# Three chained stages on one Trainium2 core: operands of the last stage at equal addresses mod 512, and its first tiles split inside the middle stage

## The chip, the cores and the metric

The kernel runs on one core of one Trainium2 chip. The metric is device time in microseconds (us) of one execution; the times of the kernel before are 1609.0, 1609.07 and 1609.45 us in three runs, with a median of 1609.07 us.

## What is computed

```python
def reference(**kwargs):
    attn_out = _attn_ref(**attn_kwargs)          # 8 x 8 heads x 576 tokens x 64
    x = attn_out.transpose(0, 2, 1, 3).reshape(B * S, H * D)      # 4608 x 512
    h = np.maximum(np.maximum(x @ w1, x @ w2), x @ w3)            # 4608 x 768
    x = (h @ w_out).astype(np.float32)                            # 4608 x 512
    h = x @ w_in                                                  # 4608 x 2048
    g = h - np.tanh(h)
    return (g @ w_out2).astype(np.float32)                        # 4608 x 512
```

The attention pools k and v by 8 along the sequence before its softmax.

## The kernel before, in words

Every float32 operand is split into a high part H, rounded to the matmul's float32r format, and a low part L, the rest. A product is then three matmuls, H by H, H by L and L by H, added up in one accumulation tile. The work has three stages.

**Stage A** (to about 628 us) is the attention, with the three products of the first block and their maximum spread between its steps. The last of its nine blocks of 384 tokens has no attention beside it. `moe_group` (L466) issues its matmuls at L476 to L478: 384 moving columns of `xH`/`xL`, weights `wH`/`wL` as the stationary operand. Its results go to DRAM as `hs`.

**Stage B** (about 628 to 790 us) multiplies `hs` by the first block's output weights `woH`/`woL` (L583 to L605). It walks over 54 tiles: 9 blocks of 512 tokens by 6 tiles of 128 rows. For each it issues 12 matmuls at L592 to L594, with 512 moving columns of `ioH`/`ioL` and slices of `wo` as the stationary operand. A block's four sums sit in four accumulation tiles, which come from the pool `psm` in even blocks and from `ps2` in odd ones; after its sixth tile they are copied to `ob` by ScalarE (L598) and VectorE (L600) in turn, and stored as `xs` (L601). `load_split` (L558) loads a tile into `ioL` (pool `io`, 8 buffers) and returns a function that casts it to `ioH` on ScalarE (L566, 7 buffers) and subtracts on the engine it was given (L567): VectorE in this stage. Beside this, `conv_c` converts the 32 weight tiles of the second block from float64 words to float32 by integer operations on VectorE (L78 to L87), a cast (L89) and a subtraction on GpSimd (L90), into `ctH`/`ctL` (pool `wl`).

**Stage C** (from about 795 us) is the second block. `h2` (L657) forms 128 rows of the hidden layer by 512 tokens from 12 matmuls (L662 to L664: moving `ioH`/`ioL`, stationary slices of `ct`). `gact` (L631) makes g = h - tanh(h) from it with four ScalarE activations, six VectorE operations, a cast to `gH` (L650) and a subtraction to `gL` (L651). `prod` (L667) multiplies g by the output weights in 12 matmuls (L675 to L677: moving `ct`, stationary slices of `gH`/`gL`) and comes three steps behind `h2` (LAG). There are 9 x 16 steps, so 3456 matmuls of 512 columns. Tiles of `xs` are loaded by `c_load` and split by `c_split`, four for each of the nine blocks, with the subtraction on GpSimd; the first four are asked for at the head of the stage (L687 to L690).

The order of instructions on each engine comes from a scheduler that places the recorded operations; it may place an operation of the text of stage C among those of stage B. The DMAs are issued by SyncE (Q), one after the other.

**Where tiles lie.** Pools on the left side take addresses from the bottom of each partition upward, pools on the right side from the top down. In the built program the left side begins with 16384 bytes of DMA scratch, 128 bytes of constants of the framework and 64 of `cst`, so `wa` and, in its place later, `wl` begin at byte 16576. The right side's pools end at byte 229344. `wH` to `xL` fill bytes 16576 to 127168 and `ct` fills 16576 to 147648, on the left; `gH`, `gL`, `ioL` and `ioH` fill 174048 to 221152, on the right. Tiles of 2048 bytes or of 512-byte pieces keep the remainder of their pool. Modulo 512 this gives: `wH`, `wL`, `xH`, `xL` 192; `woH`, `woL`, `ioH`, `ioL` 480; `ctH`, `ctL` 192; `gH`, `gL` 480. So each matmul of stages A and B has its moving and its stationary operand at equal remainders (192 with 192, 480 with 480), and each matmul of stage C has them at different ones (480 moving with 192 stationary in `h2`, 192 with 480 in `prod`).

Pools for accumulation tiles: `psm` (4 tiles) and `ps2` (4) are closed at the end of stage B, and `psc` (3 `ps_mm` for `h2` and 5 `ps_acc` for `prod`) takes their place (L608 to L610).

Of the kernel before, what the change touches and what calls it, by code (L numbers as in the profile page):

```python
# [7 lines left out]
F32 = mybir.dt.float32  # L8
# [8 lines left out]
B, NH, S, D = 8, 8, 576, 64  # L17
# [13 lines left out]
NB = NT // BB  # L31
HG = 1536
NF = FF // 128
NE = DM // 128
# [13 lines left out]
def moe_chain_kernel(ctx, tc, qt, kt, vm, vl, ident, cst, w123, wo1, win, wout, out):  # L48
    nc = tc.nc
    V, A, G, T, Q = nc.vector, nc.scalar, nc.gpsimd, nc.tensor, nc.sync  # L50
# [3 lines left out]
    def pool(name, bufs=1, side="left", **kw):  # L54
        cm = tc.tile_pool(name=name, bufs=bufs, side=side, **kw)
        stacks[name] = cm
        return cm.__enter__()
# [5 lines left out]
    psm = pool("psm", bufs=4, space=PS)  # L63
    ps2 = pool("ps2", bufs=2, space=PS)
    hs = [dr.tile([NF, 128, HG], F32, name=f"hs{i}") for i in range(NT // HG)]
    xs = [dr.tile([NE, 128, BB], F32, name=f"xs{i}") for i in range(NB)]

    # float64 words to float32, split into two float32r parts
    def conv_load(st, src):
        raw = st.tile([128, 512, 2], I32, tag="raw", name="raw", bufs=2)  # L70
        Q.dma_start(out=raw.bitcast(I64).rearrange("p n o -> p (n o)"), in_=src)
# [17 lines left out]
        A.copy(H, w)  # L89
        eng.tensor_tensor(out=L, in0=w, in1=H.bitcast(F32), op=ALU.subtract)  # L90

# [1 line left out]
    cp = pool("cst")  # L93
    wa = pool("wa")
    xr = pool("xr", bufs=3)
    hp = pool("hp", bufs=4)
    sta = pool("sta")
    at = pool("at", side="right")

    consts = cp.tile([128, 12], F32, name="consts")  # L100
# [13 lines left out]
    def zero(t):  # L114
        G.memset(t.bitcast(F32), 0.0)

    # attention units: (first token, tiles of tokens); a tile is (batch, first token in batch, count)
    units = []
    for b in range(0, B, 2):
        units += [  # L120
# [5 lines left out]
    tiles = []  # L126
# [189 lines left out]
        A.copy(h, ps[:, :n])  # L316
        V.tensor_tensor(out=l, in0=ps[:, :n], in1=h.bitcast(F32), op=ALU.subtract)  # L317

    # one list of steps for the whole attention, in the order in which they are issued
    steps = []  # L320

    def add(fn, *a):
# [55 lines left out]
    for n in range(n0, ntl + 1):  # L378
        qks, aux = [], []
        if n < ntl:  # L380
# [3 lines left out]
            k = n - first_tile[b]  # L384
# [19 lines left out]
            tail = [(av, tiles[n - 1][3], p) for p in range(NP)]  # L404
    for o in tail:
        add(*o)
    # v of a batch may be replaced once its last product is issued
    done_at = {}
    for i, (f, a) in enumerate(steps):
        if f is av and a[1] == NP - 1:  # L410
# [11 lines left out]
            f(*a)  # L422
            pos[0] += 1

    # startup
    for t in (kbd[0], VX, VH, VL, kbd[1]):
        zero(t)
    next_k()
# [58 lines left out]
    hsb = {}  # L487

    def moe_part(groups, upto):
        """groups of products, with the attention's steps up to upto spread over them"""  # L490
        first = pos[0]

        def pace(x):
            attn_to(first + (upto - first) * x // (2 * len(groups)))

        for k, (j, f, m) in enumerate(groups):
            conv_next()
            moe_group(j, f, m, lambda: pace(2 * k + 1))
            pace(2 * k + 2)
# [4 lines left out]
    HF = NF // 2  # L504

    def point(x):
        """the step at which the attention is x blocks far"""
        j = int(x)
        if j >= NA - 1:
            return len(steps) - 1  # L510
        lo = block_end[j - 1] if j else -1
        return int(lo + (block_end[j] - lo) * (x - j)) if x > j else lo
# [24 lines left out]
    for nme in ("sta", "hp", "xr", "wa"):  # L537
        close(nme)

# [1 line left out]
    wl = pool("wl")  # L541
    stb = pool("stb", side="right")
    wt = [(wl.tile([128, 512], F32R, name=f"ctH{c}"), wl.tile([128, 512], F32R, name=f"ctL{c}"))
          for c in range(2 * NC2)]
    # pairs in the order of use: input chunk c, output chunk c
    srcs = [(win if c % 2 == 0 else wout)[c // 2] for c in range(2 * NC2)]
    raws = {i: conv_load(stb, srcs[i]) for i in range(2)}
    nconv = [0]
# [9 lines left out]
    def load_split(src, eng):  # L558
        l = io.tile([128, 512], F32R, tag="L", name="ioL", bufs=8)
        r = l.bitcast(F32)  # L560
        Q.dma_start(out=r, in_=src)
        t = [None, l]

        def split():
            h = io.tile([128, 512], F32R, tag="H", name="ioH", bufs=7)
            A.copy(h, r)  # L566
            eng.tensor_tensor(out=l, in0=r, in1=h.bitcast(F32), op=ALU.subtract)  # L567
            t[0] = h

        return t, split  # L570

    def hsrc(j, kc):
        g, o = divmod(j * BB, HG)
        return hs[g][kc][:, o:o + BB]

    loads = [(j, kc) for j in range(NB) for kc in range(NF)]
    AHEAD, SPL = 4, 2
    lt = {}
# [3 lines left out]
        lt[i][1]()  # L582
    for i, (j, kc) in enumerate(loads):  # L583
        if kc == 0:
            acc = [psm.tile([128, 512], F32, tag="mm", name="ps_mm") if j % 2 == 0 else
                   ps2.tile([128, 512], F32, tag="sc" if e < 2 else "tr", name="ps_acc") for e in range(NE)]
        (h, l), _ = lt.pop(i)
        if i + SPL < len(loads):
            lt[i + SPL][1]()
        for e in range(NE):  # L590
            c = slice(e * 128, e * 128 + 128)
            T.matmul(acc[e], woH[kc][:, c], h, start=(kc == 0), stop=False)  # L592
            T.matmul(acc[e], woH[kc][:, c], l, start=False, stop=False)
            T.matmul(acc[e], woL[kc][:, c], h, start=False, stop=(kc == NF - 1))  # L594
            if kc == NF - 1:
                ob = io.tile([128, 512], F32, tag="ob", name="ob", bufs=4)
                if e % 2 == 0:
                    A.copy(ob, acc[e])  # L598
                else:
                    V.tensor_copy(ob, acc[e])  # L600
                Q.dma_start(out=xs[j][e], in_=ob)  # L601
        if i + AHEAD < len(loads):
            lt[i + AHEAD] = load_split(hsrc(*loads[i + AHEAD]), V)
        while nconv[0] < min(2 * NC2, (i + 1) * 2 * NC2 // (len(loads) - 2)):
            conv_c()  # L605
    close("stb")
# [2 lines left out]
    close("psm")  # L609
    psc = pool("psc", space=PS)  # L610

# [1 line left out]
    gp = pool("gp", bufs=2, side="right")  # L613
    xl_ = [(j, kc) for j in range(NB) for kc in range(NE)]
    lt = {}
    nld, nsp = [0], [0]

    def c_load():
        i = nld[0]
        if i < len(xl_):  # L620
            j, kc = xl_[i]
            lt[i] = load_split(xs[j][kc], G)
            nld[0] += 1

    def c_split():
        i = nsp[0]
        if i < len(xl_):
            lt[i][1]()
            nsp[0] += 1

    def gact(ps):  # L631
        u = gp.tile([128, 512], F32, tag="u", name="u")
        th = gp.tile([128, 512], F32, tag="th", name="th")
# [23 lines left out]
    def h2(j, c):  # L657
        ps = psc.tile([128, 512], F32, tag="mm", name="ps_mm", bufs=3)
        wh, wl_ = (t.rearrange("p (a b) -> p a b", b=128) for t in wt[2 * c])
        for kc in range(NE):  # L660
            xh, xl2 = lt[j * NE + kc][0]
            T.matmul(ps, wh[:, kc], xh, start=(kc == 0), stop=False)  # L662
            T.matmul(ps, wh[:, kc], xl2, start=False, stop=False)  # L663
            T.matmul(ps, wl_[:, kc], xh, start=False, stop=(kc == NE - 1))  # L664
        return ps
# [18 lines left out]
                r0 = j * BB + t * 128  # L684
                Q.dma_start(out=out[r0:r0 + 128, :], in_=ob)

    for _ in range(4):  # L687
        c_load()
    for _ in range(4):
        c_split()  # L690
    seq = [(j, c) for j in range(NB) for c in range(NC2)]
    for i in range(len(seq) + LAG):
        if i < len(seq):
            j, c = seq[i]
            ps = h2(j, c)
        if i >= LAG:
            prod(*seq[i - LAG])
        if i < len(seq):
            gs[j, c] = gact(ps)
            if c == 2:  # L700
                for _ in range(NE):
                    c_load()
            if 6 <= c < 10:
                c_split()
            if c == NC2 - 1:
                for k in range(NE):
                    lt.pop(j * NE + k)
    for nme in ("psc", "gp", "io", "wl", "cst"):
        close(nme)


# [52 lines left out]
```

## Time and profile before

| what | value |
|---|---|
| median of three runs | 1609.07 us |
| runs | 1609.0, 1609.07, 1609.45 us |
| span of the profiled execution | 1608.5 us |
| busy in it: TensorE, VectorE, ScalarE, GpSimd | 1548.1, 1215.2, 836.4, 223.7 us |
| matmuls in it | 7540 |
| DMA traffic | 117.87 MB |

The profile is of one execution. Its span (first to last instruction) is 0.6 us below the median of the runs. TensorE's row shows matmuls that overlap in the records, because each is pipelined into the next; the distance from one start to the next is what counts for the time, not the duration of one.

### The profile page before, as it was taken

What the parts mean: (1) busy time and instruction counts of PE and PEld (TensorE: products, weight loads), DVE (VectorE), ACT (ScalarE), POOL (GpSimd) and SP (SyncE); (2) the same over time, 40 slices, a digit from 0 to 9 for tenths busy, and PEclk for the clock granted to TensorE, in tenths of its full rate; (3) what the DMA queues carried; (4) which work ended last, traced back from release to release, by engine and by line L of the source; (5) the groups of instructions that cost most, each with busy time, mean ns of one, the idle gap of its engine ahead of it and who ended that gap; (6) DMA issues with size and microseconds to landing.
All of it is one profiled execution on the core that took longest, in us unless ns stands there. A gap on an engine that the chain in (4) does not pass through costs nothing.

```text
span 1608.5 us, 21497 instructions
## 1 busy us (share of the span) xinstructions
PE 1548.1 (96%) x7540; PEld 1337.7 (83%) x7540; DVE 1215.2 (76%) x2131; ACT 836.4 (52%) x2081; POOL 223.7 (14%) x245
## 2 busy tenths in 40 slices
PE   4789999999999999998899999999999999999999
PEld 4688999999999999876688888888888888888887
DVE  8999565555555663999588878788888888887886
ACT  5565455545545521444465555555555555555554
POOL 5351210202010011332301001010101001010000
PEclk9899999999999999999999999999999999999999
DMA  7455232212121232676500001010100000010000
GB/s 236 158 161 163 84 99 79 87 45 75 42 65 39 67 120 77 230 241 234 198 1 27 26 2 52 1 53 0 33 21 27 26 27 27 1 54 0 27 1 27
DMA packets 61997, 117.87 MB, mean 73 GB/s; under 512 B 10816, under 2 KB 20160, under 8 KB 61888
## 3 DMA queue, kind: packets, MB, share of 16 engines
q1 hardware_dynamic: 61888, 116.49, 21.8%
q8 instruction: 59, 0.97, 0.3%
q14 instruction: 50, 0.41, 0.1%
HBM read 83.43 MB, written 33.03 MB: 72 GB/s over the span
## 4 chain that ended last, share of the span: by engine, by line
PE 50%; DVE 0%; issue 0%
PE ps_mm L663 8%; PE ps_mm L662 8%; PE ps_mm L664 8%; PE ps_acc L676 8%; PE ps_acc L675 8%; PE ps_acc L677 8%; DVE ob L683 0%
## 5 line engine op out<-in xcount | busy, mean ns | idle before, releaser
L476 PE MATMUL ps_mm<-xH,wH 128*128 128x384 f32 x864 | 304.5, 353 | 5.3 <-ACT wH L89 4.5
L477 PE MATMUL ps_mm<-xL,wH 128*128 128x384 f32 x864 | 292.4, 339 | 1.0 <-DVE xL L317 1.0
L478 PE MATMUL ps_mm<-xH,wL 128*128 128x384 f32 x864 | 292.7, 339 | 0.6 <-POOL wL L90 0.6
L650 ACT CAST gH<-w 128x512 fp32r<-128x512 f32 x144 | 89.4, 621 | 297.0 <-DVE w L649 297.0
L662 PE MATMUL ps_mm<-ioH,ctH 128*128 128x512 f32 x576 | 228.3, 396 | 5.3 <-ACT ob L598 5.3
L663 PE MATMUL ps_mm<-ioL,ctH 128*128 128x512 f32 x576 | 229.1, 398 | 0.0
L664 PE MATMUL ps_mm<-ioH,ctL 128*128 128x512 f32 x576 | 228.5, 397 | 0.0
L675 PE MATMUL ps_acc<-ctH,gH 128*128 128x512 f32 x576 | 228.1, 396 | 0.0
L676 PE MATMUL ps_acc<-ctL,gH 128*128 128x512 f32 x576 | 227.9, 396 | 0.0
L677 PE MATMUL ps_acc<-ctH,gL 128*128 128x512 f32 x576 | 227.9, 396 | 0.0
L651 DVE TENSOR_TENSOR gL<-w,gH 128x512 fp32r<-128x512 f32 x144 | 104.1, 723 | 92.5 <-ACT gH L650 92.3
L476 PEld LDWEIGHTS ps_mm<-xH,wH 128*128 128x128 f32 x864 | 164.7, 191 | 7.2 <-ACT wH L89 4.8
L477 PEld LDWEIGHTS ps_mm<-xL,wH 128*128 128x128 f32 x864 | 164.6, 191 | 1.9 <-DVE xL L317 1.7
L478 PEld LDWEIGHTS ps_mm<-xH,wL 128*128 128x128 f32 x864 | 163.7, 189 | 1.5 <-POOL wL L90 1.5
L567 POOL TENSOR_TENSOR ioL<-ioL,ioH 128x512 fp32r<-128x512 f32 x36 | 53.5, 1509 | 666.9 <-ACT ioH L566 666.9
L662 PEld LDWEIGHTS ps_mm<-ioH,ctH 128*128 128x128 f32 x576 | 108.6, 189 | 32.2 <-ACT ob L598 5.7
L663 PEld LDWEIGHTS ps_mm<-ioL,ctH 128*128 128x128 f32 x576 | 108.7, 189 | 27.1
L664 PEld LDWEIGHTS ps_mm<-ioH,ctL 128*128 128x128 f32 x576 | 108.8, 189 | 26.0
L675 PEld LDWEIGHTS ps_acc<-ctH,gH 128*128 128x128 f32 x576 | 108.2, 188 | 26.5
L677 PEld LDWEIGHTS ps_acc<-ctH,gL 128*128 128x128 f32 x576 | 108.2, 188 | 26.5
L676 PEld LDWEIGHTS ps_acc<-ctL,gH 128*128 128x128 f32 x576 | 108.2, 188 | 25.8
L482 DVE TENSOR_TENSOR h<-h,ps_mm 128x384 f32<-128x384 f32 x144 | 79.0, 549 | 66.0 <-PE ps_mm L478 59.2
(108 smaller groups left out, 2924.9 us busy)
## 6 DMA issues: line engine op xcount, KB each, us to landing
hs<-h SPq DMA_DIRECT2D x72, 192.0 KB, 1.9
ioL<-hs SPq DMA_DIRECT2D x54, 256.0 KB, 4.2
kraw<-kt SPq DMA_DIRECT2D x32, 288.0 KB, 3.9
raw<-w SPq DMA_DIRECT2D x18, 512.0 KB, 3.5
xs<-ob SPq DMA_DIRECT2D x36, 256.0 KB, 2.6
ioL<-xs SPq DMA_DIRECT2D x36, 256.0 KB, 3.0
out<-ob SPq DMA_DIRECT2D x36, 256.0 KB, 2.2
qraw<-qt SPq DMA_DIRECT2D x32, 256.0 KB, 2.7
```

Source lines behind the costliest of these rows:

```text
L476: T.matmul(ps[:, :BA], wH[i][:, kc], xh[:, kc], start=(kc == 0), stop=False)
L477: T.matmul(ps[:, :BA], wH[i][:, kc], xl[:, kc], start=False, stop=False)
L478: T.matmul(ps[:, :BA], wL[i][:, kc], xh[:, kc], start=False, stop=(kc == NE - 1))
L482: V.tensor_tensor(out=t, in0=t, in1=ps[:, :BA], op=ALU.max)
L650: A.copy(gH, w)
L651: V.tensor_tensor(out=gL, in0=w, in1=gH.bitcast(F32), op=ALU.subtract)
L662: T.matmul(ps, wh[:, kc], xh, start=(kc == 0), stop=False)
L663: T.matmul(ps, wh[:, kc], xl2, start=False, stop=False)
L664: T.matmul(ps, wl_[:, kc], xh, start=False, stop=(kc == NE - 1))
L675: T.matmul(acc, gH[:, r], oh, start=(c == 0), stop=False)
L676: T.matmul(acc, gH[:, r], ol, start=False, stop=False)
L677: T.matmul(acc, gL[:, r], oh, start=False, stop=(c == NC2 - 1))
```

## The change

- A tile of 72 float32 (288 bytes a partition), `rpad`, is placed at the right end before all other right-side pools, and is closed last. Every right-side tile moves down by 288 bytes: modulo 512, 480 becomes 192. Nothing reads or writes it.
- The DMA scratch is set to 1024 bytes in place of 16384. Every left-side tile moves down by 15360 bytes, which is 30 x 512.
- The accumulation tiles of stage B's blocks change places: odd blocks now take `psm`, and even ones, the first and the last among them, `ps2`.
- `c_load` and `c_split` are defined ahead of stage B's loop. Its last four rounds load the first four `xs` tiles, and its last two split two each, with the subtraction on VectorE instead of GpSimd. The head of stage C no longer does so. Later loads are made as before, on GpSimd.
- The dictionary of stage C's tiles is named `ct`. Comments go.

```diff
         A.copy(H, w)
         eng.tensor_tensor(out=L, in0=w, in1=H.bitcast(F32), op=ALU.subtract)
 
     cp = pool("cst")
     wa = pool("wa")
     xr = pool("xr", bufs=3)
     hp = pool("hp", bufs=4)
     sta = pool("sta")
+    pool("rp", side="right").tile([128, 72], F32, name="rpad")
     at = pool("at", side="right")
 
     consts = cp.tile([128, 12], F32, name="consts")
...
     def hsrc(j, kc):
         g, o = divmod(j * BB, HG)
         return hs[g][kc][:, o:o + BB]
+    xl_ = [(j, kc) for j in range(NB) for kc in range(NE)]
+    ct = {}
+    nld, nsp = [0], [0]
+    def c_load(eng):
+        i = nld[0]
+        if i < len(xl_):
+            j, kc = xl_[i]
+            ct[i] = load_split(xs[j][kc], eng)
+            nld[0] += 1
+    def c_split():
+        i = nsp[0]
+        if i < len(xl_):
+            ct[i][1]()
+            nsp[0] += 1
 
     loads = [(j, kc) for j in range(NB) for kc in range(NF)]
     AHEAD, SPL = 4, 2
...
         lt[i][1]()
     for i, (j, kc) in enumerate(loads):
         if kc == 0:
-            acc = [psm.tile([128, 512], F32, tag="mm", name="ps_mm") if j % 2 == 0 else
+            acc = [psm.tile([128, 512], F32, tag="mm", name="ps_mm") if j % 2 else
                    ps2.tile([128, 512], F32, tag="sc" if e < 2 else "tr", name="ps_acc") for e in range(NE)]
         (h, l), _ = lt.pop(i)
         if i + SPL < len(loads):
...
                 Q.dma_start(out=xs[j][e], in_=ob)
         if i + AHEAD < len(loads):
             lt[i + AHEAD] = load_split(hsrc(*loads[i + AHEAD]), V)
+        else:
+            c_load(V)
+        if i >= len(loads) - 2:
+            c_split()
+            c_split()
         while nconv[0] < min(2 * NC2, (i + 1) * 2 * NC2 // (len(loads) - 2)):
             conv_c()
     close("stb")
...
     close("psm")
     psc = pool("psc", space=PS)
 
     gp = pool("gp", bufs=2, side="right")
-    xl_ = [(j, kc) for j in range(NB) for kc in range(NE)]
-    lt = {}
-    nld, nsp = [0], [0]
-    def c_load():
-        i = nld[0]
-        if i < len(xl_):
-            j, kc = xl_[i]
-            lt[i] = load_split(xs[j][kc], G)
-            nld[0] += 1
-    def c_split():
-        i = nsp[0]
-        if i < len(xl_):
-            lt[i][1]()
-            nsp[0] += 1
     def gact(ps):
         u = gp.tile([128, 512], F32, tag="u", name="u")
         th = gp.tile([128, 512], F32, tag="th", name="th")
...
         ps = psc.tile([128, 512], F32, tag="mm", name="ps_mm", bufs=3)
         wh, wl_ = (t.rearrange("p (a b) -> p a b", b=128) for t in wt[2 * c])
         for kc in range(NE):
-            xh, xl2 = lt[j * NE + kc][0]
+            xh, xl2 = ct[j * NE + kc][0]
             T.matmul(ps, wh[:, kc], xh, start=(kc == 0), stop=False)
             T.matmul(ps, wh[:, kc], xl2, start=False, stop=False)
             T.matmul(ps, wl_[:, kc], xh, start=False, stop=(kc == NE - 1))
...
                 r0 = j * BB + t * 128
                 Q.dma_start(out=out[r0:r0 + 128, :], in_=ob)
 
-    for _ in range(4):
-        c_load()
-    for _ in range(4):
-        c_split()
     seq = [(j, c) for j in range(NB) for c in range(NC2)]
     for i in range(len(seq) + LAG):
         if i < len(seq):
...
             gs[j, c] = gact(ps)
             if c == 2:
                 for _ in range(NE):
-                    c_load()
+                    c_load(G)
             if 6 <= c < 10:
                 c_split()
             if c == NC2 - 1:
                 for k in range(NE):
-                    lt.pop(j * NE + k)
-    for nme in ("psc", "gp", "io", "wl", "cst"):
+                    ct.pop(j * NE + k)
+    for nme in ("psc", "gp", "io", "rp", "wl", "cst"):
         close(nme)
 
 
...
         "w123": c(w123), "wo1": c(moe_w_out).view(np.int64).reshape(NF, 128, 512),
         "win": cols(moe2_w_in), "wout": c(moe2_w_out).view(np.int64).reshape(NC2, 128, 512),
     }
-    nc = bacc.Bacc("TRN2", target_bir_lowering=False, num_devices=1)
+    nc = bacc.Bacc("TRN2", target_bir_lowering=False, num_devices=1, dynamic_dma_scratch_size=1024)
     args = [nc.dram_tensor(n, a.shape, mybir.dt.from_np(a.dtype), kind="ExternalInput").ap()
             for n, a in arrays.items()]
     out = nc.dram_tensor("out", (NT, DM), F32, kind="ExternalOutput").ap()
```

What this makes of the order, at three places. `mk`, `u` are the first tiles of `gact`; `xs0` is the first block of what stage C reads; a number behind a name is that of the buffer's allocation, and line numbers after the change are up to 19 higher.

VectorE at the end of stage B, before:

```order
L567 TENSOR_TENSOR ioL_8375<-ioL_8375,ioH_8402 128x512
L600 COPY ob_8298<-ps_acc_8162 128x512
L600 COPY ob_8310<-ps_acc_8164 128x512
L600 COPY ob_8448<-ps_mm_8328 128x512
L600 COPY ob_8460<-ps_mm_8330 128x512
L646 TENSOR_SCALAR mk_8511<-u_8506 128x512
```

and in the changed program:

```order
L569 TENSOR_TENSOR ioL_8379<-ioL_8379,ioH_8408 128x512
L619 COPY ob_8302<-ps_mm_8166 128x512
L619 COPY ob_8314<-ps_mm_8168 128x512
L569 TENSOR_TENSOR ioL_8396<-ioL_8396,ioH_8449 128x512
L569 TENSOR_TENSOR ioL_8423<-ioL_8423,ioH_8452 128x512
L569 TENSOR_TENSOR ioL_8447<-ioL_8447,ioH_8481 128x512
L569 TENSOR_TENSOR ioL_8479<-ioL_8479,ioH_8484 128x512
L619 COPY ob_8464<-ps_acc_8332 128x512
L619 COPY ob_8476<-ps_acc_8334 128x512
L653 TENSOR_SCALAR mk_8515<-u_8510 128x512
```

The four subtractions of `xs0` stand on VectorE now, ahead of its two copies of the last block's sums (`ob`), behind which the stage C operations start.

ScalarE at the same place, before:

```order
L566 CAST ioH_8481<-ioL_8473 128x512
L566 CAST ioH_8484<-ioL_8475 128x512
L566 CAST ioH_8487<-ioL_8477 128x512
L566 CAST ioH_8490<-ioL_8479 128x512
L566 CAST ioH_8784<-ioL_8592 128x512
L566 CAST ioH_8832<-ioL_8594 128x512
L598 COPY ob_8442<-ps_mm_8327 128x512
L598 COPY ob_8454<-ps_mm_8329 128x512
L566 CAST ioH_8880<-ioL_8596 128x512
L640 ACTIVATE u_8506<-ps_mm_8493 128x512
```

and in the changed program:

```order
L568 CAST ioH_8449<-ioL_8396 128x512
L568 CAST ioH_8452<-ioL_8423 128x512
L568 CAST ioH_8481<-ioL_8447 128x512
L568 CAST ioH_8484<-ioL_8479 128x512
L568 CAST ioH_8788<-ioL_8596 128x512
L568 CAST ioH_8836<-ioL_8598 128x512
L617 COPY ob_8458<-ps_acc_8331 128x512
L617 COPY ob_8470<-ps_acc_8333 128x512
L568 CAST ioH_8884<-ioL_8600 128x512
L647 ACTIVATE u_8510<-ps_mm_8497 128x512
```

The order is the same: six casts of `xs` tiles (the last two are of block 1) stand ahead of the last block's two copies, which now read `ps_acc` in place of `ps_mm`.

SyncE, from the first load of `xs0`, before and then in the changed program:

```order
L561 DMA ioL_8473<-xs0_66 128x512
L601 DMA xs7_73<-ob_8292 128x512
L601 DMA xs7_73<-ob_8298 128x512
L601 DMA xs7_73<-ob_8304 128x512
L601 DMA xs7_73<-ob_8310 128x512
L561 DMA ioL_8475<-xs0_66 128x512
L561 DMA ioL_8477<-xs0_66 128x512
L561 DMA ioL_8479<-xs0_66 128x512
L561 DMA ioL_8592<-xs1_67 128x512
```

```order
L563 DMA ioL_8396<-xs0_66 128x512
L620 DMA xs7_73<-ob_8296 128x512
L620 DMA xs7_73<-ob_8302 128x512
L620 DMA xs7_73<-ob_8308 128x512
L620 DMA xs7_73<-ob_8314 128x512
L563 DMA ioL_8423<-xs0_66 128x512
L563 DMA ioL_8447<-xs0_66 128x512
L563 DMA ioL_8479<-xs0_66 128x512
L563 DMA ioL_8596<-xs1_67 128x512
```

The order is the same: the second to the fourth load of `xs0` stand behind the four stores of block 7.

TensorE at the first matmuls of stage C, with the semaphores each waits for, before and then in the changed program:

```order
L662 MATMUL ps_mm<-ioH,ctH_6953 128x512 [waits DMAHW3_49,DMAHW4_49,DMAHW2_49,DMAHW5_49,DMAHW1_49,DMAHW6_49,DMAHW0_49,DMAHW7_49,DVE_49,Activation_49]
L663 MATMUL ps_mm<-ioL,ctH_6953 128x512 [waits Pool_49]
L664 MATMUL ps_mm<-ioH,ctL_6954 128x512
L662 MATMUL ps_mm<-ioH,ctH_6953 128x512
L663 MATMUL ps_mm<-ioL,ctH_6953 128x512 [waits Pool_49]
```

```order
L669 MATMUL ps_mm<-ioH,ctH_6957 128x512 [waits DMAHW3_49,DMAHW4_49,DMAHW2_49,DMAHW5_49,DMAHW1_49,DMAHW6_49,DMAHW0_49,DMAHW7_49,DVE_49,Activation_49]
L670 MATMUL ps_mm<-ioL,ctH_6957 128x512
L671 MATMUL ps_mm<-ioH,ctL_6958 128x512 [waits Pool_49]
L669 MATMUL ps_mm<-ioH,ctH_6957 128x512
L670 MATMUL ps_mm<-ioL,ctH_6957 128x512
```

The first still waits for ScalarE and VectorE. The values awaited are, in both built programs, those of the last block's second copy on each of the two engines. The waits on GpSimd for the subtractions (on the second matmul of each three) are gone; those that remain are for the conversion of the weights.

## Rows read from the trace of the kernel before

**Rows 1.** The page: span, and busy time of the engines.

```profile
span 1608.5 us, 21497 instructions
...
PE 1548.1 (96%) x7540; PEld 1337.7 (83%) x7540; DVE 1215.2 (76%) x2131; ACT 836.4 (52%) x2081; POOL 223.7 (14%) x245
```

**Rows 2.** The page: chain that ended last, by engine and by line.

```profile
PE 50%; DVE 0%; issue 0%
PE ps_mm L663 8%; PE ps_mm L662 8%; PE ps_mm L664 8%; PE ps_acc L676 8%; PE ps_acc L675 8%; PE ps_acc L677 8%; DVE ob L683 0%
```

**Rows 3.** The page: groups by line, with busy, mean | idle before, releaser.

```profile
L662 PE MATMUL ps_mm<-ioH,ctH 128*128 128x512 f32 x576 | 228.3, 396 | 5.3 <-ACT ob L598 5.3
L663 PE MATMUL ps_mm<-ioL,ctH 128*128 128x512 f32 x576 | 229.1, 398 | 0.0
...
L675 PE MATMUL ps_acc<-ctH,gH 128*128 128x512 f32 x576 | 228.1, 396 | 0.0
```

**Rows 4.** Engines by stretch; (x) counts instructions in it, those under way included.

```profile
core 0: us, PE busy (x) PEld busy (x) DVE busy (x) ACT busy (x) POOL busy (x), PEclk, DMA share, GB/s
628.10:704.20 76.10, 76.10 (x337) 63.04 (x337) 70.23 (x100) 33.56 (x57) 24.55 (x16) 1.00 0.64 217
795.00:801.00 6.00, 5.79 (x14) 4.54 (x15) 0.00 (x0) 0.81 (x3) 4.00 (x4) 0.50 0.66 219
802.00:1604.00 802.00, 802.00 (x3438) 645.02 (x3438) 658.28 (x1024) 440.38 (x765) 44.81 (x29) 1.00 0.06 20
1598.00:1604.00 6.00, 6.00 (x27) 4.84 (x26) 1.45 (x3) 1.23 (x3) 0.00 (x0) 1.00 0.00 0
```

**Rows 5.** TensorE's timeline: stage A near 576 us, stage B from 628 us (start, duration).

```profile
575.77 0.33 PE L476 MATMUL ps_mm<-xH,wH 128*128 128x384 f32 x1
...
577.85 0.33 PE L476 MATMUL ps_mm<-xH,wH 128*128 128x384 f32 x1
...
628.10 0.39 PE L592 MATMUL ps_mm<-ioH,woH 128*128 128x512 f32 x1
...
704.26 0.39 PE L592 MATMUL ps_mm<-ioH,woH 128*128 128x512 f32 x1
```

**Rows 6.** TensorE's timeline: end of stage B, first and last matmuls of stage C.

```profile
789.54 0.39 PE L594 MATMUL ps_mm<-ioH,woL 128*128 128x512 f32 x1
795.21 0.79 PE L662 MATMUL ps_mm<-ioH,ctH 128*128 128x512 f32 x1 [5.27 <-ACT ob L598]
795.80 0.63 PE L663 MATMUL ps_mm<-ioL,ctH 128*128 128x512 f32 x1
...
801.34 0.41 PE L664 MATMUL ps_mm<-ioH,ctL 128*128 128x512 f32 x1
...
1598.18 0.40 PE L675 MATMUL ps_acc<-ctH,gH 128*128 128x512 f32 x1
...
1604.25 0.40 PE L677 MATMUL ps_acc<-ctH,gL 128*128 128x512 f32 x1
```

**Rows 7.** Timelines of ScalarE, VectorE, GpSimd and SyncE between the stages.

```profile
790.88 3.30 ACT L566 CAST ioH<-ioL 128x512 fp32r<-128x512 f32 x5 [6.17 <-DMA ioL<-xs]
794.09 1.07 ACT L598 COPY ob<-ps_mm 128x512 f32<-128x512 f32 x2
...
788.61 0.69 DVE L600 COPY ob<-ps_mm 128x512 f32<-128x512 f32 x1 [2.71 <-PE ps_mm L594]
789.97 0.69 DVE L600 COPY ob<-ps_mm 128x512 f32<-128x512 f32 x1 [0.67 <-PE ps_mm L594]
...
791.58 7.42 POOL L567 TENSOR_TENSOR ioL<-ioL,ioH 128x512 fp32r<-128x512 f32 x6 [5.49 <-ACT ioH L566]
...
783.74 2.88 SPq L601 DMA_DIRECT2D xs<-ob  x4
787.02 2.73 SPq L561 DMA_DIRECT2D ioL<-xs  x6
```

**Rows 8.** The subtraction of a split by engine: ns min/median/max, first and last start.

```profile
L567 DVE TENSOR_TENSOR ioL<-ioL,ioH x54: 674/684/1795, 562.0 to 784.0; 128x512 fp32r<-128x512 f32 x54
```

## The prediction

> **What bounds the kernel now.** I read the page first. TensorE is busy for 1548.1 of 1608.5 us and VectorE, the next, for 1215.2 [rows 1]. The chain that ended last is TensorE alone, in equal parts on the six matmul lines of stage C, each with 8% of the span [rows 2]. The groups by line say the same from the other side: in front of L663 and L675 TensorE never sat idle, and in front of L662 it did so once, for 5.3 us [rows 3]. So half of the span is a run of 3456 matmuls that wait for nobody, and only their own pace, or the one gap ahead of them, can shorten it.
>
> The pace is read from starts, not from durations. From 802 to 1604 us there are 3438 matmuls in the count, one of them under way at the edge: 802.00 / 3437 = 233.3 ns each, at the granted clock of 1.00, the upper of the two levels (2.4 GHz) [rows 4]. Stage B has matmuls of the same form, 512 columns by 128 x 128 weights. Its first starts at 628.10 and its 337th at 704.26 us, with the same granted clock and no stall between: 76.16 / 336 = 226.7 ns [rows 4, 5]. Against 213.3 ns for 512 columns at 2.4 GHz that is 13.4 ns on top in stage B and 20.0 ns in stage C. Stage A has 384 columns: 13 starts from 575.77 to 577.85 us are 12 steps of 173.3 ns, 13.3 on top of 160.0 [rows 5]. So the surplus is the same 13.3 to 13.4 ns for stages A and B and for two column counts, and half as much again in stage C.
>
> It is not the other engines that slow stage C. From 1598 to 1604 us DMA and GpSimd do nothing and VectorE and ScalarE have three operations each [rows 4], and the last 26 steps, from 1598.18 to 1604.25 us, still take 233.5 ns each [rows 6]. Stage B ran at 226.7 ns with VectorE busy for 70.23 of 76.10 us and the DMAs for 0.64 of it [rows 4]. Nor is it the role of an operand: `h2` moves `io` over weights as stage B does. What differs is where the operands lie. In A both remainders mod 512 are 192, in B both are 480, and in C one is 192 and the other 480. Neither remainder is slow as such, nor in either role; only the unequal pair is.
>
> **The change part by part.**
>
> The shift by 288 bytes gives both operands of every matmul of stage C the remainder 192, as in stage A. I take the price of stage B for it, 226.7 ns, because it is the nearest row (same columns, same weights, same format). No row shows a pair at equal remainders of which one lies on the left and one on the right side, so I bound it. Below, 226.7 stands too: no pair in A or B falls under 13.3 ns of surplus. Above I take a second step of 6.6 ns on the first one, 240 ns, and treat that as a rival. The first 14 matmuls of stage C run from 795.21 to 801.34 us, at the granted clock of 0.50 (1.2 GHz) [rows 4]; the 13 steps from 795.80 us take 426 ns each, 512 columns at 1.2 GHz with no surplus [rows 6], so I leave them as they are. From 801.34 to the last start at 1604.25 us there are 3441 steps in 802.91 us [rows 6], so 233.3 ns again; at 226.7 ns they take 780.1 us. **Gain: 22.8 us.**
>
> In stages A and B the shift changes no pair: right-side pools move together, and the 15360 bytes on the left are whole multiples of 512. Cost nothing. Vector operations on tiles at remainder 192 and on tiles at 480 are not told apart by any wait on the chain.
>
> The earlier split: I cost it at nothing. In the trace of before, TensorE ends stage B with the matmul that starts at 789.54 and starts stage C at 795.21 us; the 5.27 us in front are put down to ScalarE's copy of the sums, L598 [rows 6]. That copy is late because it stands behind five casts, 790.88 to 794.18 us, which waited for the loads of `xs`; two copies then take until 795.16 us [rows 7]. The loads start at 787.02 us, behind the four stores of block 7, which SyncE issues from 783.74 us [rows 7]. In the changed order SyncE has the same rows in the same places, and ScalarE has the same six casts ahead of the same two copies. The first matmul of stage C still waits for the last block's copies. That these read `ps2` now and `h2` begins in `psm`'s place does not help, since the wait is for all copies, whichever tile they read. So TensorE starts at about 795.2 us again, and its clock falls as before.
>
> What does move there is the subtraction, from GpSimd (1.24 us each, 7.42 us for six [rows 7]) to VectorE (0.68 us median [rows 8]), and with it VectorE's two last copies: at 788.61 and 789.97 us before [rows 7], now behind the subtraction of the last `xs0` tile. Its cast is the third of the five, done at about 790.88 + 3 x 0.66 = 792.9 us; the subtraction ends at 793.6 and two copies of 0.69 us at 795.0 us. That is 0.2 us ahead of ScalarE's copies, which therefore still set the start. If GpSimd's own subtraction for block 1 gets in the way and one takes the longest of its 54 times, 1.8 us [rows 8], TensorE starts 0.9 us late. I keep that as the upper bound of this term.
>
> The exchange of `psm` and `ps2` in the other blocks costs nothing: TensorE went from stage A into B without a gap with the old choice. At the faster pace VectorE needs 658.28 us [rows 4] out of 779 instead of 802 us, 84% instead of 82%: it does not become the bound.
>
> **Sum.** 1608.5 - 22.8 = 1585.7 us of span. The median of the runs lies 0.57 us above the span of the profiled execution, so I say **1586.3 us**, 1.4% faster. A measurement of this kernel can tell about 0.2%, 3.2 us, from no change.
>
> **The rivals.**
>
> *The addresses do not matter.* Then stage C keeps 233.3 ns, from some other cause (say, one operand on the left side and one on the right, as in C alone), and the time stays at 1609 us, within 0.9 us. For it: only stage C mixes the sides, so the rows cannot separate side from remainder. Against it: a side is only an end of one address range, and stage A's tiles, spread over 110 KB of it, show the small surplus, while stage C's, some of them within 30 KB of each other, show the large one. The Trainium skill speaks for this rival: "SBUF — State Buffer", section "SBUF: two separate sides", says that inside the engine side only the port pair shared by VectorE and GpSimd causes contention and that TensorE never waits on anyone, and knows no rule on addresses. By that page the sum would be 1609 us; by the rows, where the same matmul takes 226.7 and 233.3 ns at one clock, 1586 us, and the rows decide for me. Chance 0.10.
>
> *The gap closes as well.* If the first tiles are ready when stage B ends and the wait for ScalarE's copies does not hold, TensorE saves the 5.3 us [rows 3] and the half clock: 14 matmuls in 6.13 us instead of 14 x 0.2267 = 3.17 us. Together 8.3 us more, so 1578.0 us. Against it stands the order on SyncE and ScalarE. Chance 0.09.
>
> *Equal remainders across the sides are dearer still.* If mixing the sides is what costs 6.6 ns and equal remainders in both put the two reads on each other again, each of 3441 matmuls pays a second step, 240 ns: 3441 x 6.6 = 22.7 us more, 1631.8 us. It decides as soon as the pace of stage C exceeds 233.3 ns. Nothing in A or B hints at it. Chance 0.04.
>
> *Half of it.* Only one of `h2` and `prod` reaches 226.7 ns: 1597.7 us. Chance 0.03.
>
> **How the numbers follow.** The forecast keeps 0.74, within 1585 to 1588.5 us. With the closed gap that is 0.83, so the range is 1577.5 to 1588.5 us. Faster: 0.74 + 0.09 + 0.03 = 0.86; same 0.10; slower 0.04.
>
> **What would show it.** Starts of stage C's matmuls 226.7 ns apart at clock 1.00, a first matmul of stage C some 5.3 us after the last of B with ScalarE's copies as its releaser, four subtractions of about 0.7 us on VectorE just ahead, and last starts near 1581.4 us. I am wrong if the pace is still 233 ns, or if the gap ahead of stage C is under 3 us.

## The result, and the profile after

The changed kernel takes 1584.2 us (median of its runs), against 1609.07 us before: the ratio of the two is 0.9841, with a 95% interval of 0.9823 to 0.9859. (Ratios below are to runs of the kernel before in the same measurement, with their interval in brackets.) The forecast was 1586.3 us in a range of 1577.5 to 1588.5 us. The one profiled execution of this first measurement ran at a lower granted clock (0.78 in the mean) and took 1827.38 us, against 1583.07 and 1584.2 us for the two others, so the profile after is that of the same kernel's next run, `e1_changed`, 1585.18 us in the median.

The page of that run, answering to [rows 1] and [rows 3]: span, busy time of the engines, and the groups of stage C (busy, mean | idle before, releaser). The lines of `h2` are L669 to L671 now, those of `prod` L682 to L684.

```profile
span 1582.8 us, 21496 instructions
...
PE 1526.3 (96%) x7540; PEld 1339.5 (85%) x7540; DVE 1211.0 (77%) x2135; ACT 833.5 (53%) x2081; POOL 220.4 (14%) x241
...
L669 PE MATMUL ps_mm<-ioH,ctH 128*128 128x512 f32 x576 | 225.4, 391 | 5.3 <-ACT ob L617 5.3
L670 PE MATMUL ps_mm<-ioL,ctH 128*128 128x512 f32 x576 | 225.2, 391 | 0.0
...
L682 PE MATMUL ps_acc<-ctH,gH 128*128 128x512 f32 x576 | 224.1, 389 | 0.0
```

The span is 25.7 us shorter with the same 7540 matmuls. In front of L669 TensorE sat idle once, for the same 5.3 us, with the same releaser, ScalarE's copy of the last sums. The mean duration of a matmul's record fell by 5 to 7 ns, from 396 to 398 ns down to 389 to 391 ns, about as much as the pace below.

The stretches that answer to [rows 4]:

```profile
core 0: us, PE busy (x) PEld busy (x) DVE busy (x) ACT busy (x) POOL busy (x), PEclk, DMA share, GB/s
624.10:700.20 76.10, 76.10 (x338) 63.00 (x337) 69.86 (x100) 33.47 (x57) 24.11 (x16) 1.00 0.64 216
792.36:798.40 6.04, 6.04 (x14) 4.78 (x15) 0.00 (x0) 0.85 (x2) 2.14 (x2) 0.50 0.63 217
799.00:1578.00 779.00, 779.00 (x3438) 645.05 (x3437) 652.80 (x1025) 438.06 (x765) 45.40 (x29) 1.00 0.06 21
```

and TensorE's timeline, answering to [rows 6]:

```profile
786.70 0.39 PE L613 MATMUL ps_acc<-ioH,woL 128*128 128x512 f32 x1
792.36 0.79 PE L669 MATMUL ps_mm<-ioH,ctH 128*128 128x512 f32 x1 [5.28 <-ACT ob L617]
792.96 0.63 PE L670 MATMUL ps_mm<-ioL,ctH 128*128 128x512 f32 x1
...
798.50 0.42 PE L671 MATMUL ps_mm<-ioH,ctL 128*128 128x512 f32 x1
...
1578.51 0.39 PE L684 MATMUL ps_acc<-ctH,gL 128*128 128x512 f32 x1
```

The same 3438 matmuls that filled 802.00 us before [rows 4] fill 779.00 us now: 779.00 / 3437 = 226.7 ns each, at the same granted clock of 1.00 (2.4 GHz). That is 23.0 us. Ahead of them the picture is the old one: 5.3 us idle, then the clock at 0.50 (1.2 GHz), 13 steps of 426 ns from 792.96 to 798.50 us, as in [rows 6].

**Where the 25.7 us are.** Stage B's first matmul starts at 624.12 us (628.10 before [rows 5]): 4.0 us. Stage B lasts 162.6 us to its last start (161.4 before): 1.1 us lost. From there to stage C's first start it is 5.66 us both times. From stage C's first start to its last it is 786.15 us (809.05 before): 22.9 us. The tail is 4.3 us both times. The change accounts for the 22.9 us. The 4.0 us come up in stage A: 2.9 us of them stand by its 600th matmul, some 156 us in, and most of the rest comes after its 3000th. In the nine profiles of other kernels below, stage B starts anywhere from 625.81 to 628.10 us. In `e4_b_unequal` nothing of stage A is changed, and it starts at 626.17 us, so some 2 us are scatter from one execution to the next; that the other 2 us are so too is not shown. The medians of the runs taken beside `e1_changed` differ by 23.6 us (1608.82 and 1585.18 us).

### The profile page after: what moved, and what is told of

Read it like the earlier page. It is cut to its first block, busy times and chain, and to the rows that moved or that the text cites. A ratio compares the mean times of both kernels' runs of the same rounds, so it can differ in the third digit from the quotient of the medians.

```text
span 1825.6 us, 21496 instructions
## 1 busy us (share of the span) xinstructions
PE 1790.5 (98%) x7540; PEld 1437.7 (79%) x7540; DVE 1227.9 (67%) x2135; ACT 841.4 (46%) x2081; POOL 215.5 (12%) x241
## 4 chain that ended last, share of the span: by engine, by line
PE 94%; DVE 4%; DMA 1%; POOL 1%; issue 0%; SPq 0%; ACT 0%; DVEq 0%; POOLq 0%
PE ps_mm L478 9%; PE ps_mm L480 9%; PE ps_mm L479 9%; PE ps_mm L669 8%; PE ps_mm L670 8%; PE ps_acc L682 8%; PE ps_acc L683 8%; PE ps_mm L671 8%; PE ps_acc L684 8%; PE ps_acc L611 2%; PE ps_acc L613 2%; PE ps_acc L612 2%; PE ps_mm L612 2%; PE ps_mm L613 2%; PE ps_mm L611 1%; PE ps_sc L242 1%
## 5 line engine op out<-in xcount | busy, mean ns | idle before, releaser
L478 PE MATMUL ps_mm<-xH,wH 128*128 128x384 f32 x864 | 343.3, 398 | 3.1 <-ACT wH L89 3.1
L480 PE MATMUL ps_mm<-xH,wL 128*128 128x384 f32 x864 | 336.6, 390 | 0.4 <-POOL wL L90 0.4
L479 PE MATMUL ps_mm<-xL,wH 128*128 128x384 f32 x864 | 335.8, 389 | 0.0
L669 PE MATMUL ps_mm<-ioH,ctH 128*128 128x512 f32 x576 | 250.0, 434 | 0.8 <-ACT ioH L568 0.8
L683 PE MATMUL ps_acc<-ctL,gH 128*128 128x512 f32 x576 | 250.5, 435 | 0.0
L682 PE MATMUL ps_acc<-ctH,gH 128*128 128x512 f32 x576 | 250.4, 435 | 0.0
L670 PE MATMUL ps_mm<-ioL,ctH 128*128 128x512 f32 x576 | 249.7, 434 | 0.0
L671 PE MATMUL ps_mm<-ioH,ctL 128*128 128x512 f32 x576 | 248.9, 432 | 0.0
L684 PE MATMUL ps_acc<-ctH,gL 128*128 128x512 f32 x576 | 248.7, 432 | 0.0
L647 ACT ACTIVATE u<-ps_mm 128x512 f32<-128x512 f32 x144 | 86.0, 597 | 159.4 <-PE ps_mm L671 159.4
L669 PEld LDWEIGHTS ps_mm<-ioH,ctH 128*128 128x128 f32 x576 | 111.4, 193 | 42.6 <-ACT ioH L568 1.4
L684 PEld LDWEIGHTS ps_acc<-ctH,gL 128*128 128x128 f32 x576 | 112.9, 196 | 39.8
L671 PEld LDWEIGHTS ps_mm<-ioH,ctL 128*128 128x128 f32 x576 | 111.8, 194 | 41.1
L653 DVE TENSOR_SCALAR mk<-u 128x512 uint8<-128x512 f32 x144 | 61.3, 426 | 123.0 <-ACT u L647 122.6
L682 PEld LDWEIGHTS ps_acc<-ctH,gH 128*128 128x128 f32 x576 | 112.8, 196 | 39.8
```

Source lines behind the costliest of these rows:

```text
L478: T.matmul(ps[:, :BA], wH[i][:, kc], xh[:, kc], start=(kc == 0), stop=False)
L479: T.matmul(ps[:, :BA], wH[i][:, kc], xl[:, kc], start=False, stop=False)
L480: T.matmul(ps[:, :BA], wL[i][:, kc], xh[:, kc], start=False, stop=(kc == NE - 1))
L647: A.activation(u, ps, AF.Square)
L682: T.matmul(acc, gH[:, r], oh, start=(c == 0), stop=False)
L683: T.matmul(acc, gH[:, r], ol, start=False, stop=False)
```

## The experiments

The theory: stage C's pace hangs on the addresses of the two operands modulo some power of two, and nothing else in the change does anything. The rivals: the sides count (one operand left, one right); or the earlier split and the exchange of `psm` and `ps2` among stage B's blocks (the exchange, for short) bring the time.

**The two halves of the change, each alone.** First the changed kernel itself.

> The changed kernel itself, for a profile at the granted clock of 1.00. If equal remainders are the whole gain: stage C's 3441 steps at 226.7 ns, the gap in front of stage C still about 5.3 us with ScalarE's copies as its releaser, about 1586 us. If the gap closes too: first matmul of stage C within 2 us of the last of stage B, about 1578 us. The runs so far, 1583 to 1584 us, lie between the two, so a gap of some 2 to 3 us would not surprise.

Measured: 1585.18 us, ratio 0.985 [0.9834, 0.9867]. Its profile is the one above.

Then the kernel before with the unused tile alone:

```diff
     sta = pool("sta")
+    pool("rp", side="right").tile([128, 72], F32, name="rpad")
     at = pool("at", side="right")
...
-    for nme in ("psc", "gp", "io", "wl", "cst"):
+    for nme in ("psc", "gp", "io", "rp", "wl", "cst"):
```

> The kernel before with the 288-byte pad on the right side alone, scratch, order of splits and accumulation tiles as before. Remainder theory: stage C at 226.7 ns and 22.8 us less than before, about 1586 us; the gap stays at 5.3 us. Sides theory (one operand left, one right is what costs): stage C stays at 233.3 ns, 1609 us.

Measured: 1586.07 us, ratio 0.9856 [0.9841, 0.9871]. And the changed kernel without that tile and with the old scratch size:

```diff
-    pool("rp", side="right").tile([128, 72], F32, name="rpad")
...
-    for nme in ("psc", "gp", "io", "rp", "wl", "cst"):
+    for nme in ("psc", "gp", "io", "wl", "cst"):
...
-    nc = bacc.Bacc("TRN2", target_bir_lowering=False, num_devices=1, dynamic_dma_scratch_size=1024)
+    nc = bacc.Bacc("TRN2", target_bir_lowering=False, num_devices=1)
```

> The changed kernel without pad and without the smaller scratch: the early split and the exchange of accumulation tiles alone. If they are worth nothing, as predicted: 1609 us within 1, stage C at 233.3 ns, gap 5.3 us. If they close part of the gap: 2 to 8 us less than before, 1601 to 1607 us.

Measured: 1609.58 us, ratio 1.0001 [0.9991, 1.001]. The same stretch of stage C, 760 us long, in the profile of the tile alone:

```profile
810.00:1570.00 760.00, 760.00 (x3355) 629.51 (x3354) 638.54 (x1002) 426.67 (x746) 45.36 (x29) 1.00 0.06 21
```

and in that of the split alone:

```profile
810.00:1570.00 760.00, 760.00 (x3259) 611.23 (x3258) 627.35 (x975) 417.86 (x726) 44.78 (x29) 1.00 0.06 21
```

TensorE, VectorE and ScalarE start some 3% more instructions in the first, and TensorE is full in both: 760 / 3354 = 226.6 ns against 760 / 3258 = 233.3 ns. So 288 unused bytes are the whole gain. The split and the exchange are worth nothing within 0.1%; the smaller scratch was not run by itself, but with it and these two the time is that of the tile alone (1585.18 and 1586.07 us, with intervals that overlap).

**Sides or remainders.** The kernel before, with 288 unused bytes on the right side between `io` and `wo`, so that stage B's weights lie at another remainder than its moving tiles, both still on the right side; closed before stage C:

```diff
+    pool("wp", side="right").tile([128, 72], F32, name="wpad")
...
+    close("wp")
```

> The kernel before with a 288-byte pad between the pools io and wo, both on the right side: stage B's pairs now lie on one side at unequal remainders (480 moving, 192 stationary); stage C as before. Remainder theory: the dense part of stage B (336 steps from 628 us) at 233.3 ns instead of 226.7, 2.2 us more there, of which stage B's later stalls may take some back. Sides theory: stage B stays at 226.7 ns.

Measured: 1609.35 us, ratio 1.0004 [0.9993, 1.0014]. TensorE's timeline in stage B, its first matmul and its 325th (start, duration):

```profile
626.16 0.39 PE L593 MATMUL ps_mm<-ioH,woH 128*128 128x512 f32 x1
...
701.76 0.39 PE L593 MATMUL ps_mm<-ioH,woH 128*128 128x512 f32 x1
```

75.60 us / 324 = 233.3 ns at the granted clock of 1.00, where stage B before has 226.7 ns [rows 5]. With `e2_pad_alone`, in which a pair across the sides is fast, this ends the theory of the sides: an equal pair is fast on one side and across both, an unequal pair is slow on one side and across both. The time shows little of it, because stage B is not full later on: its 648 matmuls should pay 4.3 us more, and from its first start to its last it takes 163.3 instead of 161.4 us. The waits for the splits take up part of the rest: they add up to 7.8 us in this stage B, against 9.0 us before from 700 us on alone.

**Which difference is cheap.** The changed kernel with other sizes of the unused tile, one line each:

```diff
-    pool("rp", side="right").tile([128, 72], F32, name="rpad")
+    pool("rp", side="right").tile([128, 8], F32, name="rpad")
```

with 8 as here (difference 256), 56 (difference 64), 64 (difference 32) and 40 (difference 128 bytes modulo 512).

> The changed kernel with a pad of 32 bytes in place of 288: right-side tiles at remainder 448, left-side ones at 192, so stage C's pairs differ by 256 mod 512. If the remainder mod 512 must be equal: stage C at 233.3 ns, about 1608 us. If a coarser rule holds, equal remainders mod 64, 128 or 256: 226.7 ns, about 1585 us.

> The changed kernel with a pad of 224 bytes: right side at remainder 256, a difference of 64 mod 512. If equality mod 512 (or 128, or 256) is needed: 233.3 ns, about 1608 us. If mod 64 is enough: 226.7 ns, about 1585 us.

> The changed kernel with a pad of 256 bytes: right side at remainder 224, a difference of 32 mod 512, so remainders mod 64 differ as in the kernel before (288 is 32 mod 64), though the addresses are close. If mod 64 (or any coarser equality) is what counts: 233.3 ns, about 1608 us. If only mod 32 counted it would be 226.7 ns, which the kernel before already speaks against.

> The changed kernel with an unused tile of 160 bytes instead of 288 on the right side, so that the two operands of stage C's matmuls differ by 128 bytes modulo 512. If equality modulo 128 is enough (that 0 and 256 were cheap and 32, 64, 224 and 288 dear speaks for it as much as for the next), stage C goes at 226.7 ns and the run takes about 1586. If it has to be equality modulo 256, 233.3 ns and about 1608. A value between the two would say that the price is graded.

Measured: 1586.26 us at 256, 1607.53 us at 64 and 1608.51 us at 32 (one run each, where seven runs of the kernel before beside them took 1606.89 to 1611.68 us), and 1605.92 us at 128, ratio 0.9984 [0.9974, 0.9995]. The stretch from 810 to 1570 us (us, TensorE's busy time and count, granted clock, DMA), for 256:

```profile
810.00:1570.00 760.00, 760.00 (x3355) 1.00 0.06 21
```

for 64:

```profile
810.00:1570.00 760.00, 760.00 (x3270) 1.00 0.06 21
```

for 32:

```profile
810.00:1570.00 760.00, 760.00 (x3258) 1.00 0.06 21
```

and for 128:

```profile
810.00:1570.00 760.00, 760.00 (x3263) 1.00 0.06 21
```

| difference modulo 512, bytes | ns per step in stage C |
|---|---|
| 0 (changed kernel) | 226.7 |
| 256 | 226.7 |
| 128 | 233.0 |
| 64 | 232.5 |
| 32 | 233.3 |
| 288 (before) | 233.3 |

So of the differences tried it is equality modulo 256 that is cheap, not modulo 128, and 512 in the change's description is more than is needed. It is the difference, not the place of the right-side tiles as such: in stage B of the three dear kernels both operands lie at the moved remainder (320, 256 and 224), and its first 324 steps take 226.7 ns each. The dear paces are means of uneven steps. In the changed kernel the steps of this stretch are 226 or 227 ns, at 256 they are 225 to 228 ns; before they are 229 to 236 ns, and at 128 they fall into two groups, 228 to 230 ns and 234 to 239 ns. Between the dear means there is 0.8 ns, 2.9 us over stage C at most. The kernel with difference 128 is the one among them whose time is clearly below before's, by 2.3 us; its pace is worth 1 us of that. In its profile only 6 of stage C's first steps are at the half clock (granted 0.50), against 14 before, which at 0.2 us each is worth 1.6 us there; whether its other runs had as few is not known.

**The gap ahead of stage C.** It did not close, as forecast. That it is held open by the closing of `psm` and `ps2` and the opening of `psc` in their place was argued from the order alone, so it was tried: in the changed kernel `psm` and `ps2` are not closed after stage B, and stage C takes its tiles from them.

```diff
-    close("ps2")
-    close("psm")
-    psc = pool("psc", space=PS)
...
-        ps = psc.tile([128, 512], F32, tag="mm", name="ps_mm", bufs=3)
+        ps = psm.tile([128, 512], F32, tag="mm", name="ps_mm")
...
-                accs[j, t] = psc.tile([128, 512], F32, tag="acc", name="ps_acc", bufs=5)
+                accs[j, t] = ps2.tile([128, 512], F32, tag="sc" if t < 2 else "tr", name="ps_acc")
```

> The changed kernel without closing psm and ps2 ahead of stage C: h2 takes psm's four tiles, prod ps2's four instead of five. The first matmul of stage C then waits for its own tile and operands alone. If the wait for all of the last block's copies makes the gap: the first three matmuls follow stage B at once, the rest wait for the casts of the second to the fourth tile, some 1.5 to 2 us of idle time in all instead of 5.3, and the clock may not fall (2.9 us more): 4 to 7 us less than the changed kernel, about 1579 us. If the late loads alone make the gap: no change, 1585 us. Four accumulation tiles in place of five may cost stalls at the eight changes of block, up to 0.7 us each.

Measured: 1579.29 us, ratio 0.9812 [0.9794, 0.983]. TensorE's timeline at the border:

```profile
788.70 0.39 PE L613 MATMUL ps_acc<-ioH,woL 128*128 128x512 f32 x1
788.93 0.39 PE L666 MATMUL ps_mm<-ioH,ctH 128*128 128x512 f32 x1
789.15 0.39 PE L667 MATMUL ps_mm<-ioL,ctH 128*128 128x512 f32 x1
789.38 0.39 PE L668 MATMUL ps_mm<-ioH,ctL 128*128 128x512 f32 x1
790.65 0.50 PE L666 MATMUL ps_mm<-ioH,ctH 128*128 128x512 f32 x1 [0.88 <-ACT ioH L568]
791.38 0.50 PE L667 MATMUL ps_mm<-ioL,ctH 128*128 128x512 f32 x1 [0.22 <-DVE ioL L569]
```

and the engines there, with the granted clock behind the busy times:

```profile
788.00:798.00 10.00, 8.89 (x38) 6.77 (x37) 5.91 (x9) 7.83 (x15) 3.80 (x3) 1.00 0.79 267
```

The first tile of `xs0` was split by 785.8 us, 3 us earlier; the first three matmuls follow the last of stage B in its own step of 0.23 us. What is left is 0.88 us for the next tile's cast and 0.22 us for its subtraction, and the granted clock stays at 1.00. Against `e1_changed` the way from the last start of stage B to the last start of stage C is 785.4 instead of 791.8 us, 6.4 us less. So the 5.28 us were a wait for the new pool; without it 1.1 us of waits for data come up, and this version beats both kernels. The four accumulation tiles in place of five cost no more than one later wait of 0.06 us in stage C. Here the earlier split should be worth something, since it has the first tile ready; that was not run by itself.

**Can the rest go too?** In that version, the four early loads four rounds sooner and the splits two rounds sooner:

```diff
-        else:
+        if len(loads) - 8 <= i < len(loads) - 4:
             c_load(V)
-        if i >= len(loads) - 2:
+        if len(loads) - 4 <= i < len(loads) - 2:
             c_split()
```

> The version with the middle stage's PSUM pools kept for stage C, and in it the four early loads of stage C's first tiles issued at steps 46 to 49 and split at steps 50 and 51, four and two steps sooner. If the 0.88 us wait for ScalarE's cast of the fourth tile that is left there comes from the late load, the idle at the stages' border falls under 0.4 us and the time is 0.5 to 1 us below that version's, 1578.5 or so: too little to be sure of. A rival: the last loads of the middle stage now stand behind block 7's stores on SP, and TensorE waits up to 3 us for them inside stage B; then the time is 1580 to 1582.

Measured: 1584.55 us, ratio 0.9851 [0.9832, 0.987]. The rival came, dearer than priced. (The 0.88 us were a wait for the second tile, as the rows above show, not for the fourth, as this expectation has it.) TensorE's timeline:

```profile
787.97 0.39 PE L613 MATMUL ps_acc<-ioH,woL 128*128 128x512 f32 x1
790.18 0.50 PE L611 MATMUL ps_acc<-ioH,woH 128*128 128x512 f32 x1 [1.82 <-ACT ioH L568]
790.90 0.50 PE L612 MATMUL ps_acc<-ioL,woH 128*128 128x512 f32 x1 [0.23 <-DVE ioL L569]
...
791.54 0.63 PE L611 MATMUL ps_acc<-ioH,woH 128*128 128x512 f32 x1
791.96 0.63 PE L612 MATMUL ps_acc<-ioL,woH 128*128 128x512 f32 x1
...
794.88 0.39 PE L613 MATMUL ps_acc<-ioH,woL 128*128 128x512 f32 x1
795.11 0.40 PE L666 MATMUL ps_mm<-ioH,ctH 128*128 128x512 f32 x1
```

and the timelines of ScalarE and SyncE there:

```profile
789.51 2.97 ACT L568 CAST ioH<-ioL 128x512 fp32r<-128x512 f32 x5 [5.57 <-DMA ioL<-hs]
...
781.92 2.79 SPq L620 DMA_DIRECT2D xs<-ob  x4
785.14 0.32 SPq L563 DMA_DIRECT2D ioL<-xs  x1
785.57 0.40 SPq L563 DMA_DIRECT2D ioL<-hs  x1
```

Stage C starts without a gap at 795.11 us, and stage B pays for it. The load of the last `hs` tile is issued at 785.57 us, behind block 7's four stores, ScalarE's cast waits for it, and the last 12 matmuls of stage B wait 1.82 us for it. From 791.54 us on most of them run at the granted clock of 0.50, in steps of 426 to 427 ns. All waits of stage B together are 3.7 us longer than in `e8_pools_kept` (13.2 and 9.5 us), and it takes 168.0 us from first to last start instead of 161.9 us: the wait moved across the border, and the clock fell there.

## Why the prediction was right

The mechanism came out as forecast: the pace of stage C is the gain, and the gap stays. The number has luck in it. The forecast's own band was 1585 to 1588.5 us; the measured 1584.2 us lies below that, in the part of the range that was there for a closed gap, and the gap did not close. `e1_changed`, the same kernel, is at 1585.18 us, and `e2_pad_alone` at 1586.07 us. One term of the sum, the 0.57 us from span to median, sets one execution against the median of others: in every run from the changed kernel on, a time lies 1.7 to 1.9 us above its own span. That would have made the forecast 1.2 us longer; in the profile of `e1_changed` the earlier start of stage B, which was not forecast, hides it.

- **The pace and its price.** The forecast took 226.7 ns for stage C from stage B and 22.8 us for 3441 steps. Measured: 226.7 ns, and 22.9 us from stage C's first to its last start. `e2_pad_alone` shows it without the rest of the change (24.2 us there, since 8 steps in place of 14 are at the half clock). The bound above, 240 ns for equal remainders across the sides, came nowhere.
- **That the sides do not matter** was argued from the spread of stage A's tiles, which is thin. `e4_b_unequal` shows it: the same side, unequal remainders, 233.3 ns. The rule cited for the rival (the Trainium skill, "SBUF — State Buffer", section "SBUF: two separate sides": TensorE's port never waits on anyone) would leave the time at 1609 us; the runs do not agree, since the same matmul at the same granted clock takes 226.7 or 233.3 ns with its operands' addresses alone changed. The measurement decides about the pace. Whether TensorE waits for the memory or its own two reads get in each other's way is not shown by any run, so why the difference counts stays open.
- **The gap stays.** 5.28 us idle with ScalarE's copy as releaser were measured and 5.3 forecast (not the 2 to 3 us that the expectation of `e1_changed` held possible), and the clock fell for 14 matmuls, as before. The 14 is partly luck: after idles of 4.8 to 5.7 us the nine profiles with a gap have from 6 (`e9_diff128`) to 14 steps at the half clock. `e8_pools_kept` shows the reason to be the one given, that the first matmul waits for all copies of the last block. The rival in which the gap closes had its price nearly right: 8.3 us, of which `e8_pools_kept` gained 6.4 us, since 1.1 us of waits for the second tile came in and slowed the steps next to them.
- **VectorE's copies against ScalarE's.** Forecast: VectorE's two copies end 0.2 us ahead of ScalarE's. Timelines of ScalarE, VectorE, GpSimd and SyncE of `e1_changed`, answering to [rows 7]:

```profile
787.75 1.28 ACT L568 CAST ioH<-ioL 128x512 fp32r<-128x512 f32 x2 [5.90 <-DMA ioL<-xs]
789.39 1.94 ACT L568 CAST ioH<-ioL 128x512 fp32r<-128x512 f32 x3 [0.37 <-DMA ioL<-xs]
791.24 1.07 ACT L617 COPY ob<-ps_acc 128x512 f32<-128x512 f32 x2
...
790.04 0.69 DVE L569 TENSOR_TENSOR ioL<-ioL,ioH 128x512 fp32r<-128x512 f32 x1 [0.29 <-ACT ioH L568]
790.65 1.28 DVE L619 COPY ob<-ps_acc 128x512 f32<-128x512 f32 x2
...
790.76 3.74 POOL L569 TENSOR_TENSOR ioL<-ioL,ioH 128x512 fp32r<-128x512 f32 x3 [10.07 <-ACT ioH L568]
...
780.86 2.90 SPq L620 DMA_DIRECT2D xs<-ob  x4
784.19 2.75 SPq L563 DMA_DIRECT2D ioL<-xs  x6
```

VectorE ends at 791.93 us, ScalarE at 792.31, and TensorE starts at 792.36: 0.4 us instead of 0.2 us ahead, the same order. The subtraction took 0.69 us and was over when GpSimd's first one started, at 790.76 us; VectorE's two copies, 1.28 us together, ran beside GpSimd's and were no slower. So the bound of 0.9 us was not needed. A small thing was missed: the five casts that ran in one piece before [rows 7] now stand 0.37 us for a load between the second and the third (0.58 us in `e3_split_alone`). Start to start, the gap is 5.67 to 6.12 us in the six kernels that have this order and open `psc`, and 5.18 to 5.66 us in the three that have the old order (before, `e2_pad_alone`, `e4_b_unequal`). That is some 0.5 us more in the mean, where nothing was forecast, from one profile each. It is not shown that the split is the cause: `e8_pools_kept` has it too and runs the five casts in one piece, in 3.29 us. Why the third load lands later was not tried.
- **Stages A and B unchanged.** Their paces are; the start of stage B is not, and with it the last start of stage C lies at 1578.5 us instead of the 1581.4 us named. That comes from stage A, as told above, and no run shows it to be part of the change: `e2_pad_alone`, with stage B from 627.14 us, has its last start at 1579.26 us.

## What to carry to other kernels

Where TensorE is full, read the step from start to start for each stage and compare stages with the same matmul: 6.6 ns in 226.7 are invisible in the busy share, and 3456 matmuls make 23 us of them. If a stage is dearer, compare the addresses of its two operands, and try an unused tile of some bytes on one side, which costs no time. Here 288 and 32 bytes brought the gain and 160, 224 and 256 did not, so work out the remainders first; only this form of matmul was tried. For a gap between stages, look at what the first matmul waits for before its data are moved: here a new pool waited for every copy of the old ones, and loads made earlier moved the wait into the stage ahead, because a load that was due sooner came to stand behind the stores.

## What was not expected of the hardware

- The pace of these matmuls (float32r, 512 columns, 128 x 128 weights) hangs on the difference of the operands' addresses modulo 256: 226.7 ns at 0 and 256 modulo 512, 232.5 to 233.3 ns at 32, 64, 128 and 288. The change's own words, equal modulo 512, were taken for the condition in the prediction; half of that is enough.
- At the granted clock of 0.50 no such surplus shows: the first steps of stage C take 426 to 427 ns with an equal pair (`e1_changed`) and with an unequal one (before, [rows 6]), 512 columns at 1.2 GHz and nothing on top.
- An idle of 1.82 us at the end of stage B (`e10_early_loads`), with shorter ones around it (0.26 and 0.88 us before, 0.23 us behind), was followed by a fall of the granted clock to 0.50. In `e8_pools_kept` idles of 0.88 and 0.22 us at the border, and of up to 1.39 us within stage B, were not followed by a fall.
